# Retention, then a GEMM pair with ELU: eight weight sums and four scalings of v on VectorE instead of GpSimd

## The chip, the cores and the metric

The kernel runs on one core of a Trainium2 chip. The metric is the device time of one execution in microseconds (us), as the median over several executions. A smaller number is better. The engines are written as in the profile: PE is TensorE (matmul), PEld its weight load, DVE is VectorE, ACT is ScalarE, POOL is GpSimd, and SP issues the DMAs. L740 is line 740 of the kernel before.

## What is computed

```python
# q, k, v: (4 batches, 8 heads, 768 tokens, 64), all fp32
gamma = 1.0 - 2.0 ** (-5.0 - np.arange(H))
for t in range(S):
    state = gamma[None, :, None, None] * state + np.einsum('bhd,bhe->bhde', k[:, :, t], v[:, :, t])
    y[:, :, t] = scale * np.einsum('bhd,bhde->bhe', q[:, :, t], state)
x = y.transpose(0, 2, 1, 3).reshape(3072, 512)
h = x @ w_in                                         # w_in: 512 x 2048
g = np.where(h > 0.0, h, np.exp(np.minimum(h, 0.0)) - 1.0)
out = g @ w_out                                      # w_out: 2048 x 512
```

## The kernel before

The 3072 tokens are worked on in six blocks of 512 (`tb` 0 to 5). For each block the retention part makes x in chunks of 128 tokens (four to a block), then a first GEMM with `w_in` and ELU makes g, and a second GEMM with `w_out` makes the output. The first block multiplies plainly in its first GEMM; all later GEMMs use Strassen's scheme with seven products of half-size matrices, and some of these products are split once more into seven. Schedules are written out by hand: Python generators emit a few instructions at each `next`, and each engine executes its own in the order in which they were emitted.

The change lies in the first GEMM of the second block (`tb` = 1), at 135 to 190 us. `first(n)` (L728) makes column block n of four. Its order comes from `strassen` (L698): product 1 (bank a, copied by ACT at L690), product 2 (bank b, read by DVE at L695, which gives C11), 6 (a, copied), 7 (bank d), 5 (a, copied; DVE reads bank d and gives C22), then 3 (C12) and 4 (bank d, read by DVE, C21). A product is eight matmuls as the profile counts them. Bank a has two buffers, b and d one each. The loop over n interleaves neighbours: products 1 and 2 of n+1 go ahead of products 3 and 4 of n (`tail`), and 6, 7 and 5 of n+1 follow. Each result passes through `elu`: two steps on ACT (L477, L478) and one on DVE (L481), which is put off by one result. After C12 two DVE differences follow (L752).

Besides, DVE makes sums for later use in this loop, a step at a time: `combine_w_in` (L674), for the first GEMM's weights, in the loop's `sides`; and `combine_w_out` (L647), whose results `wi` are sent to memory. `combine_small(j)` (L810) makes four sums of weight quarters for product j = 2 or 3 of the first GEMM of the third and later blocks, where that product is itself split in seven ("M2" and "M3"). It makes them on POOL (L816), M2 after n = 0 and M3 after n = 2, into a tile `wi` of the pool `stage`, whose three buffers it shares with `combine_w_out` and the earlier weight loads. M3 needs all that `combine_w_in` makes. `hold` (L112) is a 1x1 copy on POOL that makes the tile wait for other data. `send_small` (L641) then queues the DMAs of these tiles on SP; M2 and M3 take one DMA of 1 MB each.

`load(m)` (L99) brings chunk m of q, k and v: the loop loads chunk 8 + n at its top, for the third block. `scale_v(m)` (L275) multiplies the v part by a power of gamma (L281): on DVE for chunks 0 and 1, on POOL for all others. The four chunks of the third block are scaled after the loop. Behind the loop `stage` is closed, and `ring` takes over its memory: 11 tiles `wq` of quarter weights that `fetch_small` (L791; DMAs at L799 and L804) brings from memory for the second GEMM (L953) and for the split products of later blocks (L865).

Of the kernel before, what the change touches and what calls it, by code (L numbers as in the profile page):

```python
# [18 lines left out]
def kernel(  # L19
# [32 lines left out]
    nc = tc.nc  # L52
# [12 lines left out]
    CPB = TB // C  # L65
# [33 lines left out]
    def load(m, parts=1):  # L99

        if m >= NCHUNK:
            return
        t = ldpool.tile([P, 2048], FP32, name="chunk", tag="chunk")
        raw[m] = (
            t[:, 0:1024].rearrange("p (a h c) -> p a h c", a=2, c=C),
            t[:, 1024:2048].rearrange("p (a h d) -> p a h d", a=2, d=D),
        )
        for part in range(parts):
            c = slice(part * 2048 // parts, (part + 1) * 2048 // parts)
            nc.sync.dma_start(t[:, c], qkv[m, :, c])  # L110

    def hold(t, other):  # L112

        if other is not None:
            nc.gpsimd.tensor_copy(t[0:1, 0:1], other[0:1, 0:1])
# [6 lines left out]
    w_a, w_b, w_s = ([x[:, n] for n in range(NQ)] for x in (w_a_, w_b_, w_s_))  # L122
# [100 lines left out]
    for h in range(H):  # L223
# [11 lines left out]
        out=causal, in_=causal, compare_op=ALU.is_gt, fill=1.0, base=0, pattern=[[-1, P]], channel_multiplier=1  # L235
# [36 lines left out]
    carry = [const.tile([P, HP, D], FP32, name=f"carry{n}") for n in range(2)]  # L272
    held = {}

    def scale_v(m):  # L275
        if m >= NCHUNK:
            return
        i = chunks[m][1]
        qk, kv = raw[m]
        eng = nc.vector if m < 2 else nc.gpsimd  # L280
        eng.tensor_tensor(  # L281
            out=kv[:, 1], in0=kv[:, 1], in1=vf[:, i].unsqueeze(2).to_broadcast([C, H, D]), op=ALU.mult
        )
# [80 lines left out]
    def outputs(tb, pp):  # L364

        y = [ps_r.tile([P, 2 * 2, 2, D], FP32, name="y", tag="r") for _ in range(2)]
        for x in range(2):
            for j in range(4):
                pt = raw[tb * CPB + 2 * pp + j // 2][0][:, 1].rearrange("p h c -> p (h c)")
                within(tb, pp, x, j, y, lambda p: pt[:, (x * HP + p) * D :][:, 0:D])  # L370
        for other in range(2):
            if not other:
                yield
            else:

                for sub in range(2):
                    seen = epool.tile([P, 8], FP32, name="seen", tag="seen")
                    nc.vector.tensor_copy(seen.rearrange("p (j x) -> p j x", x=2), y[sub][:, :, :, 0])
                yield
            for x in range(2):  # L380
                across(tb, pp, x, other, y)
        i = chunks[tb * CPB + 2 * pp][1]
        for sub in range(2):
            nc.vector.tensor_tensor(
                out=place_of(x_of(tb)[:, :, 2 * pp * C : 2 * (pp + 1) * C])[:, :, :, sub, :], in0=y[sub],
                in1=place_of(powers[:, :, i * C : (i + 2) * C])[:, :, :, sub, :], op=ALU.mult,
            )
# [26 lines left out]
    def outputs_of_first():  # L414

        y = [bank(x).rearrange("p a (b x d) -> p (a b) x d", b=2, x=2) for x in "bd"]
        for x in range(2):
            for j in range(4):
                pt = raw[x][0][:, 1].rearrange("p h c -> p (h c)")
                within(0, 0, x, j, y, lambda p: pt[:, ((j // 2) * HP + p) * D :][:, 0:D])  # L420
            yield
            across(0, 0, x, 0, y)
            for sub in range(2):
                if not fresh(0, 2 * x + sub):
                    seen = epool.tile([P, 8], FP32, name="seen", tag="seen")
                    nc.vector.tensor_copy(seen[:, 0:4], y[sub][:, :, x, 0])
            if x:
                yield
            across(0, 0, x, 1, y)
            if x:  # L430
                yield
            for sub in range(2):
                nc.vector.tensor_tensor(
                    out=place_of(xb[:, :, 0 : 2 * C])[:, :, x, sub, :], in0=y[sub][:, :, x],
                    in1=place_of(powers[:, :, 0 : 2 * C])[:, :, x, sub, :], op=ALU.mult,
                )
            if not x:
                yield
# [141 lines left out]
    def small_of_pieces(at):  # L580

        sources = [
            (decoded[2 * NQ + n].rearrange("p r (d c) -> p (r d) c", d=2)[:, 1:4], sums[n])
            for n in (2 * at, 2 * at + 1)
        ]
        return combine_w_out(at, *sources)
# [54 lines left out]
    def send_small():  # L641
        while to_send:
            nc.sync.dma_start(*to_send.pop(0))
# [84 lines left out]
    def first(n):  # L728

        a11, a12, s1, a22 = w_a[n][:, :, 0], w_a[n][:, :, 1], w_b[n][:, :, 0], w_b[n][:, :, 1]  # L730
        s2, s3, s4 = (w_s[n][:, j] for j in range(3))
        b11, b12, b21, b22 = (x_of(1)[:, 2 * r : 2 * r + 2, half[t]] for r in range(2) for t in range(2))
        t1, t2, t3, t4_ = xt1
        pairs = {1: (a11, b11), 2: (a12, b21), 3: (s4, b22), 4: (a22, t4_), 5: (s1, t1), 6: (s2, t2), 7: (s3, t3)}

        def product(j, ps, begin):
            w, x = pairs[j]
            for fi in range(2):
                for j2 in range(2):
                    nc.tensor.matmul(  # L740
                        ps[:, fi, :], lhsT=w[:, fi, j2, :], rhs=x[:, j2, :],
                        start=(begin and fi == 0 and j2 == 0), stop=(j2 == 1), skip_group_check=True,
                    )

        mine = lambda name: gq[name][:, 2 * n : 2 * n + 2, :]

        def use(name, h):
            flat = lambda x: x.rearrange("p a b -> p (a b)")
            elu(flat(mine(name)), flat(h))
            if name == "C12":  # L750

                sub = lambda o, x, y: nc.vector.tensor_tensor(out=o, in0=x, in1=y, op=ALU.subtract)  # L752
                later.append(lambda: sub(mine("T3"), mine("C22"), mine("C12")))
                later.append(lambda: sub(mine("T1"), mine("C12"), mine("C11")))

        return strassen(product, use, None)
# [50 lines left out]

    W_IN = {2: w_a_[:, :, :, 1], 3: w_s_[:, :, 2]}

    def combine_small(j, behind=None):  # L810

        t = stage.tile([P, 4, 4, P], FP32, name="wi", tag="stage")
        hold(t.rearrange("p k f d -> p (k f d)"), behind)
        a11, a12, a21, a22 = (W_IN[j][:, 2 * r : 2 * r + 2, :, c, :] for r in range(2) for c in range(2))
        s1, s2, s3, s4 = (t[:, k].rearrange("p (n f) c -> p n f c", f=2) for k in range(4))
        tt = lambda o, x, y, op: nc.gpsimd.tensor_tensor(out=o, in0=x, in1=y, op=op)  # L816
        tt(s1, a21, a22, ALU.add)
        tt(s2, s1, a11, ALU.subtract)
        tt(s3, a11, a21, ALU.subtract)
        tt(s4, a12, s2, ALU.subtract)  # L820
        to_send.append((scratch3[j - 1], t.rearrange("p k f d -> p (k f d)")))

# [289 lines left out]
    sc = [ps_r.tile([P, 2, HP, D], FP32, name="sc", tag="r") for _ in range(2)]  # L1112
    score_products(sc, 0, 0, 0)
    scale_v(0)
    mask_pair(sc, 0)
    unread(1, TH)
# [3 lines left out]
    y = outputs_of_first()  # L1120
# [7 lines left out]
    take()  # L1128
    take()
    scale_v(1)  # L1130
    mask_pair(sc, 1)
    inner = plain_first()
# [10 lines left out]
    take()  # L1143
    state_sum(kvs, 0, 0, 1, 1)
    scale_v(2)
    scale_v(3)
    prepare(2, by_vector=True)
# [12 lines left out]
    y = outputs(0, 1)  # L1160
# [9 lines left out]
    def run(steps):  # L1170
        for _ in steps:
            pass
# [8 lines left out]
    def some(steps, count):  # L1181
        for _ in itertools.islice(steps, count):
            pass

    for n, _ in enumerate(inner):
# [19 lines left out]
        elif n == 12:  # L1205
            smalls = small_of_pieces(0)
# [12 lines left out]
    for n in second_of_first():  # L1219
# [6 lines left out]
        elif n == 1:  # L1226
            smalls = small_of_pieces(1)
# [48 lines left out]
    sides = [  # L1276
        itertools.chain(combine_w_in(1), last), itertools.chain(combine_w_in(2), combine_w_in(3)), iter(()), iter(()),
    ]
    smalls = [2], [], [3], []
    for n in range(NQ):  # L1280
        load(2 * CPB + n)
        cur = first(n)
        for at in range(3):
            next(cur)

        for _ in tail:
            pass
        for s in cur:
            next(sides[n], None)
            next(sides[n], None)  # L1290
            if s == "gap":
                break
        for _ in sides[n]:
            pass
        tail = cur
        for j in smalls[n]:
            combine_small(j, w_s[1].rearrange("p s a b c -> p (s a b c)") if j == 2 else None)
        send_small()
    for m in range(2 * CPB, 3 * CPB):
        scale_v(m)  # L1300

    early.close()
    ring = ctx.enter_context(tc.tile_pool(name="ring", bufs=RING))
# [14 lines left out]
    for s in sec:  # L1318
        if s == "first":
            step += 1  # L1320
        at = (step, s if s in ("first", "middle") else "end")
# [7 lines left out]
    for tb in range(2, NTB):  # L1329
# [25 lines left out]
        for at, j in enumerate(TWICE):  # L1355
            cur = first_twice(tb, j)
# [120 lines left out]
```

## Time and profile before

| | |
|---|---|
| median of 3 runs (635.6 to 638.48) | 635.99 us |
| the profiled execution | 636.29 us |
| its span, first to last instruction | 634.4 us |
| start of the first product of the changed GEMM | 135.40 us |
| start of the second GEMM's first product | 182.14 us |
| start of the first split product in the third block's first GEMM (L865) | 244.25 us |

Busy time by stretch, from the same execution (us from the span's start; us of busy time):

| stretch | what runs | PE | DVE | ACT | POOL |
|---|---|---|---|---|---|
| 0 to 87.21 | first block's retention and first GEMM | 83.77 | 67.95 | 60.62 | 9.54 |
| 87.21 to 135.40 | first block's second GEMM | 48.19 | 42.20 | 16.05 | 0.00 |
| 135.40 to 190.30 | second block's first GEMM, start of its second | 53.73 | 44.80 | 26.28 | 17.49 |
| 190.30 to 244.25 | second block's second GEMM | 53.95 | 41.47 | 8.07 | 0.00 |
| 244.25 to 634.40 | the other four blocks | 387.10 | 285.33 | 141.87 | 13.53 |

A busy engine isn't necessarily the one that sets the pace of a stretch. In lists in order of time, a line has the start, the duration, the engine, the line of code, the operation with output and inputs, the shapes, and how many instructions are merged (x8); the bracket gives idle time ahead of it and the instruction that ended it. Merged durations run from the first start to the last end. In lists of waits a line has the waiter, what it waited for, the total in us, how often, and the longest.

### The profile page before, as it was taken

To read this page: it belongs to the slowest core of one execution; us is meant where nothing else is said; L and a number is where in the kernel's file an instruction comes from. 1 tells how busy PE (TensorE), PEld (TensorE's weight loads), DVE (VectorE), ACT (ScalarE), POOL (GpSimd) and SP (SyncE) were. 2 spreads that over 40 slices of the span, in tenths; PEclk is the share of its full clock that TensorE was granted. 3 is DMA by queue.
4 is the path that set the end of the run, shared out by engine and by line. 5 is a ranking of instruction groups with operands and counts; after the bars stand their busy time and mean duration, and the time that the engine had idled before them with its cause. 6 is when DMAs were issued, how large, how long until landed. Compare 5 with 4: busy or idle time off the path is not lost.

```text
span 634.4 us, 16149 instructions
## 1 busy us (share of the span) xinstructions
PE 626.7 (99%) x6680; PEld 560.7 (88%) x6680; DVE 481.7 (76%) x870; ACT 252.9 (40%) x472; POOL 40.6 (6%) x40
## 2 busy tenths in 40 slices
PE   8999999999999999999999999999999999999998
PEld 5764568888899999889999989999988999988997
DVE  5779979978879685589676598867489878558975
ACT  6599635014551113554112556111465311366311
POOL 1111000003600000200000100000110000000000
PEclk9999999999999999999999999999999999999999
DMA  8698867687477778504889701789820697700794
GB/s 336 264 390 307 269 205 222 189 248 258 176 239 228 242 254 272 239 2 135 277 267 312 290 4 55 258 283 286 302 100 4 218 299 236 238 24 2 231 309 158
DMA packets 75897, 136.85 MB, mean 216 GB/s; under 512 B 6320, under 2 KB 31792, under 8 KB 70704
## 3 DMA queue, kind: packets, MB, share of 16 engines
q1 hardware_dynamic: 75824, 135.82, 64.2%
q8 instruction: 53, 0.87, 0.5%
q14 instruction: 20, 0.16, 0.1%
HBM read 114.56 MB, written 21.23 MB: 214 GB/s over the span
## 4 chain that ended last, share of the span: by engine, by line
PE 94%; DVE 4%; issue 1%; ACT 0%; DVEq 0%
PE pa L953 20%; PE pa L911 10%; PE pd L953 10%; PE pb L953 5%; PE pa L865 5%; PE pb L911 4%; PE pa L521 3%; PE qa L911 3%; PE x L611 3%; PE pa L740 2%; PE pd L865 2%; PE qd L911 2%; PE pd L911 2%; PE pa L611 2%; PE y L394 2%; PE kv L338 2%
## 5 line engine op out<-in xcount | busy, mean ns | idle before, releaser
L961 ACT COPY ms<-pa 128x128 f32<-128x128 f32 x104 | 27.6, 265 | 147.1 <-PE pa L953 143.7
L953 PE MATMUL pa<-ts,wq 128*128 128x128 f32 x560 | 74.2, 275 | 0.0
L953 PE MATMUL pd<-ts,wq 128*128 128x128 f32 x552 | 73.6, 276 | 0.1
L953 PEld LDWEIGHTS pa<-ts,wq 128*128 128x128 f32 x560 | 68.5, 192 | 0.4
L953 PEld LDWEIGHTS pd<-ts,wq 128*128 128x128 f32 x552 | 67.1, 192 | 0.9 <-DVE res L965 0.5
L953 PE MATMUL pa<-gC,wq 128*128 128x128 f32 x480 | 64.6, 278 | 0.0
L478 ACT ACTIVATE r<-r 128x512 f32<-128x512 f32 x96 | 60.5, 631 | 3.0
L953 PEld LDWEIGHTS pa<-gC,wq 128*128 128x128 f32 x480 | 59.0, 192 | 1.3
L477 ACT ACTIVATE r<-gC 128x512 f32<-128x512 f32 x64 | 39.9, 624 | 32.0 <-DVE gC L919 32.0
L965 DVE TENSOR_TENSOR res<-pd,ms 128x128 f32<-128x128 f32 x68 | 19.4, 286 | 39.6 <-PE pd L953 38.4
L281 POOL TENSOR_TENSOR chunk<-chunk,vf 128x512 f32<-128x512 f32 x22 | 26.3, 1199 | 318.4 <-DMA chunk<-in_qkv_dram 153.5
L481 DVE SCALAR_TENSOR_TENSOR gC<-r,gC 128x512 f32<-128x512 f32 x64 | 44.3, 724 | 0.7 <-ACT r L478 0.7
L827 DVE TENSOR_TENSOR ts<-gC,ts 128x512 f32<-128x512 f32 x60 | 41.3, 688 | 1.0
L827 DVE TENSOR_TENSOR ts<-gC 128x512 f32<-128x512 f32 x60 | 40.9, 682 | 0.0
L953 PE MATMUL pb<-gC,wq 128*128 128x128 f32 x240 | 31.7, 275 | 0.0
L986 ACT COPY res<-pa 128x128 f32<-128x128 f32 x34 | 9.0, 265 | 55.1 <-PE pa L953 55.1
L953 PEld LDWEIGHTS pb<-gC,wq 128*128 128x128 f32 x240 | 29.2, 192 | 0.0
L690 ACT COPY m<-pa 128x512 f32<-128x512 f32 x24 | 13.9, 581 | 30.1 <-PE pa L911 14.2
L919 DVE TENSOR_TENSOR gC<-qa,gC 128x512 f32<-128x512 f32 x8 | 5.5, 692 | 25.1 <-PE qa L911 18.3
L911 PE MATMUL pa<-xt,w_s 128*128 128x256 f32 x96 | 23.0, 382 | 0.0
L911 PE MATMUL pa<-xt,w_b 128*128 128x256 f32 x96 | 23.0, 382 | 0.0
L965 DVE TENSOR_TENSOR res<-res 128x512 f32<-128x512 f32 (+1 forms) x31 | 20.6, 666 | 3.0 <-DVE res L965 0.5
(256 smaller groups left out, 1258.4 us busy)
## 6 DMA issues: line engine op xcount, KB each, us to landing
wq<-scratch_dram SPq DMA_DIRECT2D x277, 256.0 KB, 4.2
chunk<-in_qkv_dram SPq DMA_DIRECT2D x23, 1024.0 KB, 8.3
wraw<-in_w_dram SPq DMA_DIRECT2D x15, 1024.0 KB, 6.1
out_dram<-res SPq DMA_DIRECT2D x14, 256.0 KB, 3.8
scratch_dram<-gT SPq DMA_DIRECT2D x12, 256.0 KB, 4.2
scratch_dram<-m SPq DMA_DIRECT2D x12, 192.0 KB, 5.6
scratch_dram<-so SPq DMA_DIRECT2D x4, 512.0 KB, 4.8
scratch_dram<-wi SPq DMA_DIRECT2D x2, 1024.0 KB, 5.1
```

The costliest lines, as they stand in the source:

```text
L281: eng.tensor_tensor(out=kv[:, 1], in0=kv[:, 1], in1=vf[:, i].unsqueeze(2).to_broadcast([C, H, D]), op=ALU.mult)
L477: nc.scalar.activation(e, h, AF.Relu, scale=-1.0)
L478: nc.scalar.activation(e, e, AF.Exp, scale=-1.0)
L481: nc.vector.scalar_tensor_tensor(g, e, -1.0, h, ALU.add, ALU.max)
L521: nc.tensor.matmul(hp, lhsT=w[n][:, fi, j // 2, j % 2, :], rhs=xb[:, j, :], start=(j == 0), stop=(j == 3))
L611: nc.tensor.matmul(X[j][:, d, :], lhsT=w[j][:, d * P : d * P + P], rhs=x[j], start=(n == 0 and d == 0), stop=at_end, skip_group_check=True,)
L827: sub = lambda o, x, y: nc.vector.tensor_tensor(out=o, in0=x, in1=y, op=ALU.subtract)
L865: nc.tensor.matmul(ps[:, f, :], lhsT=lhs[f], rhs=xs[j][k], start=(begin and f == 0), stop=True, skip_group_check=True,)
L911: nc.tensor.matmul(ps[:, fi, :], lhsT=w[:, fi, j2, :], rhs=x[:, j2, :], start=(j in (1, 7) and fi == 0 and j2 == 0), stop=(j2 == 1), skip_ ...
L953: nc.tensor.matmul(ps, lhsT=w[:, f, :], rhs=ts[j][k][:, f, :], start=(begin and f == 0), stop=(f == 3), skip_group_check=True,)
L961: nc.scalar.copy(m, ps)
L965: nc.vector.tensor_tensor(out=o, in0=x, in1=y, op=ALU.add)
```

## The change

`combine_small` becomes a generator that yields after each of its first three sums, and its sums run on DVE; the `hold` copy goes. `scale_v` gets a switch that chooses DVE, and the four scalings for the third block move from behind the loop into its last turn. The steps are placed as follows: M2's first sum ahead of the loop, its second and third in turn n = 0, its fourth in turn 1; M3's first in turn 2 ahead of `tail`, its second and third later in that turn, its fourth at the turn's end; chunk 8's v in turn 3 ahead of `tail`, chunks 9 to 11 later in that turn. M2's DMA is thereby queued at the end of turn 1 and not of turn 0. Scalings of later blocks stay on POOL.

```diff
-    def scale_v(m):
+    def scale_v(m, by_vector=False):
...
-        eng = nc.vector if m < 2 else nc.gpsimd
+        eng = nc.vector if by_vector or m < 2 else nc.gpsimd
...
-    def combine_small(j, behind=None):
+    def combine_small(j):
 
         t = stage.tile([P, 4, 4, P], FP32, name="wi", tag="stage")
-        hold(t.rearrange("p k f d -> p (k f d)"), behind)
...
-        tt = lambda o, x, y, op: nc.gpsimd.tensor_tensor(out=o, in0=x, in1=y, op=op)
+        tt = lambda o, x, y, op: nc.vector.tensor_tensor(out=o, in0=x, in1=y, op=op)
         tt(s1, a21, a22, ALU.add)
+        yield
         tt(s2, s1, a11, ALU.subtract)
+        yield
         tt(s3, a11, a21, ALU.subtract)
+        yield
         tt(s4, a12, s2, ALU.subtract)
         to_send.append((scratch3[j - 1], t.rearrange("p k f d -> p (k f d)")))
...
-    smalls = [2], [], [3], []
+    smalls = {2: combine_small(2), 3: combine_small(3)}
+    some(smalls[2], 1)
     for n in range(NQ):
         load(2 * CPB + n)
         cur = first(n)
         for at in range(3):
             next(cur)
 
+        if n in (1, 2):
+            some(smalls[n + 1], 1)
+        elif n == 3:
+            scale_v(2 * CPB, True)
         for _ in tail:
             pass
-        for s in cur:
+        for at, s in enumerate(cur):
             next(sides[n], None)
             next(sides[n], None)
+            if at == 1 and n in (0, 2):
+                some(smalls[2 if n == 0 else 3], 2)
+            elif at == 1 and n == 3:
+                for m in range(1, CPB):
+                    scale_v(2 * CPB + m, True)
             if s == "gap":
                 break
         for _ in sides[n]:
             pass
         tail = cur
-        for j in smalls[n]:
-            combine_small(j, w_s[1].rearrange("p s a b c -> p (s a b c)") if j == 2 else None)
+        if n in (1, 2):
+            run(smalls[n + 1])
         send_small()
-    for m in range(2 * CPB, 3 * CPB):
-        scale_v(m)
```

## What is predicted, before the run

> **What bounds the kernel now.** I read the page's busy shares first, then the waits of TensorE, then the order of time of each engine in the stretch that the change touches (135 to 190 us), and the waits of the SP queue last.
>
> ```profile
> span 634.4 us, 16149 instructions
> PE 626.7 (99%) x6680; PEld 560.7 (88%) x6680; DVE 481.7 (76%) x870; ACT 252.9 (40%) x472; POOL 40.6 (6%) x40
> ```
>
> TensorE is busy for 99% of the span, and the chain that ended last is PE for 94%. So nothing that DVE or POOL saves counts by itself; only time in which TensorE stands idle in the touched stretch can be won. The PE waits name it:
>
> ```profile
> PE pd L740 <- DVE h L695: 1.2, 2, 0.7
> ```
>
> and the order of time of PE shows both places (start us, us, then engine, line, operation; the bracket is idle time and its releaser):
>
> ```profile
> 149.21 1.89 PE L740 MATMUL pd<-xb,w_b 128*128 128x256 f32 x8
> 150.94 1.89 PE L740 MATMUL pa<-xb,w_s 128*128 128x256 f32 x8
> 153.56 1.99 PE L740 MATMUL pd<-xb,w_s 128*128 128x256 f32 x8 [0.73 <-DVE h L695]
> 155.38 1.96 PE L740 MATMUL pa<-xb,w_b 128*128 128x256 f32 x8
> ...
> 164.09 1.89 PE L740 MATMUL pa<-xb,w_s 128*128 128x256 f32 x8
> 166.42 1.99 PE L740 MATMUL pd<-xb,w_s 128*128 128x256 f32 x8 [0.44 <-DVE h L695]
> 168.25 1.96 PE L740 MATMUL pa<-xb,w_b 128*128 128x256 f32 x8
> ```
>
> An undisturbed product of eight matmuls starts 1.727 us after the one before (149.21 to 150.94). The product `pd` is product 7 of column block n=1 (then n=2): it needs bank d, which frees when DVE has read product 4 of the block before (L695). It starts 2.62 us after its predecessor instead of 1.73, and the two products behind it come 0.09 and 0.07 late: 1.05 us. The second place costs 0.60 + 0.10 + 0.07 = 0.77 us. Check over the whole GEMM: its first product starts at 135.40, the second GEMM's first at 182.14; 26 products lie between, 26 x 1.727 = 44.90, and 46.74 - 44.90 = 1.84 us. That is all TensorE loses there: 0.29% of the span.
>
> Why DVE is late is in the same stretch:
>
> ```profile
> 145.63 1.73 POOL L816 TENSOR_TENSOR wi<-w_a 128x512 f32<-128x512 f32 x1
> 146.14 1.63 DVE L647 TENSOR_TENSOR wi<-w_s 128x384 f32<-128x384 f32 x1
> 147.31 1.58 POOL L816 TENSOR_TENSOR wi<-w_a,wi 128x512 f32<-128x512 f32 x1
> 147.81 1.51 DVE L647 TENSOR_TENSOR wi<-wi,w_s 128x384 f32<-128x384 f32 x1
> 149.24 0.54 DVE L647 TENSOR_TENSOR wi<-w_s 128x384 f32<-128x384 f32 x1
> ...
> 162.70 3.07 DVE L481 SCALAR_TENSOR_TENSOR gC<-r,h 128x512 f32<-128x512 f32 x2
> 165.69 0.68 DVE L695 TENSOR_TENSOR h<-pd,m 128x512 f32<-128x512 f32 x1
> 166.29 0.67 DVE L481 SCALAR_TENSOR_TENSOR gC<-r,pa 128x512 f32<-128x512 f32 x1
> ```
>
> The same 128x384 operation takes 1.63 and 1.51 us while a POOL sum runs and 0.54 us once POOL is done; the pair of L481 takes 3.07 us beside POOL sums (two of 0.69 elsewhere). The last two lines, one operand in PSUM, run beside POOL at full speed. These stretched operations stand right ahead of the two late reads of bank d.
>
> **What the Trainium skill says.** GPSIMD Engine Reference, "8. Key points": POOL shares its SBUF interfaces with VectorE, and contends with DVE instructions that have two SBUF inputs. The trace agrees, down to the PSUM exception just shown. The same page, "4.1 Engine selection", puts two-input elementwise work on POOL at about half DVE's speed; here the L816 sums take 1.27 to 1.73 us on POOL and the like L674 sums 0.69 on DVE. VectorE: DVE Perf Modes, "The TRN2 errata", gives an fp32 tensor_tensor as (N+151)/0.96 ns, 691 ns for 512; the trace has 0.68 to 0.69, starting 0.60 us apart when independent and 0.72 when one needs the last.
>
> **The change part by part.** Removed: one 1x1 copy, eight POOL sums, and four POOL scalings in this stretch (L281 at 168.09 to 176.57). With them goes what they cost DVE: 1.63-0.54, 1.51-0.54, 3.07-1.28, L752 1.69 and 1.41 against 0.69, L481 1.10 and 1.30 against 0.68: 6.6 us of DVE time. Added on DVE: 12 instructions of 0.60 to 0.72, some 8 us. DVE's total stays about level; what counts is where the pieces stand. I replay DVE with PE at 1.727 us a product (starts without the stalls: product 3 of n=0 147.48, 4 149.21, 6 of n=1 150.94, 7 152.67; for n=2 one block later 159.57, 161.30, 163.03, 164.75).
> - First sum of M2, before the loop's first product is added up: DVE idles 1.18 us before 139.12. Free.
> - Its second and third: DVE idles 1.66 us before 144.85, waiting for ACT; two cost 1.3. Free.
> - Four L647 then run 146.1 to 148.15 (4 x 0.46 to 0.57) instead of to 150.25. The read of product 2 (`h<-pb`) moves from 150.17 to 148.15. ACT needs 1.36 us for its two ELU steps (150.88 to 152.17 before), during which DVE does one L481 and the fourth M2 sum (to 150.0). The L481 that waits for ACT runs at 150.2 to 150.9, so DVE is free when product 4 ends at about 151.2, reads it by 151.9, and product 7 can start at 152.67 with some 0.6 us to spare. First stall gone: 1.05.
> - n=2: the L674 sums end at about 160.4, `h<-pb` at 161.0, L481, first M3 sum to 162.1, L481 behind ACT to 163.0, `h<-pd` 163.25 to 163.95, needed at 164.75. Second stall gone: 0.77, with 0.7 to spare.
> - Second and third M3 sums follow the L752 pair, ahead of an `h<-pd` that waits for ACT: nothing queued behind them is needed by TensorE at once.
> - Fourth M3 sum stands behind that `h<-pd`. ACT's copy of product 5 starts 0.2 us after it (168.41), the read 0.62 later (169.03), L481 169.64, the sum 170.25 to 170.95. POOL had ended M3 at 168.13. This is the one step that becomes later.
> - Four scalings of v: one behind an L481 in an ACT wait, three behind L752 at about 178.0, the last needing its chunk. Chunk 11's load stands behind M3's send in SP, so it is issued at about 171.35 and lands 6.9 us later as before (168.53 to 175.5), at 178.3; DVE gets to it at 179.2. The next `h<-pd` waits for ACT until about 181.1. Free, 1.2 us to spare.
> - SP: M2's send falls behind one chunk load instead of ahead of it; M2 is first multiplied at 244 us (L865), so no one waits. M3's send moves 168.16 to about 170.98, and what stands behind it counts:
>
> ```profile
> 168.16 0.33 SPq L643 DMA_DIRECT2D scratch_dram<-wi  x1
> 168.53 0.42 SPq L110 DMA_DIRECT2D chunk<-in_qkv_dram  x1
> 173.01 0.80 SPq L804 DMA_DIRECT2D wq<-scratch_dram  x2
> ...
> SPq L804 <- DMA scratch_dram<-wi: 3.9, 1, 3.9
> ```
>
> The ring of `wq` weights lies over the `stage` buffers, so the first fetch waits until M3's send has landed: 173.01, 4.85 us after its issue; that fetch lands 4.4 us later (the DMA view of that moment), at 177.4. TensorE first loads it at 181.9: a cover of 4.5 us. After: 170.98 + 4.85 + 4.4 = 180.23, while TensorE would want it at 181.9 - 1.84 = 180.06. The cover is used up, a new stall of about 0.2 us. The second fetch is 0.37 behind and lands after some 4.8, at 181.0, just when wanted; the third is wanted only at 185.5.
>
> Sum: -1.05 - 0.77 + 0.2 = -1.6 us. The profiled execution took 636.29 us (span 634.4 and 1.9 around it) and so becomes 634.7; the median shown, 635.99, is 0.3 under that execution, so I state 634.4. Nothing after 190 us is touched: from there the order on PE, ACT and DVE is the same, and what is won moves through to the end.
>
> **Rivals.**
> - A, the new wait takes it back. If M3's send comes 1 to 2 us later than I reckon, TensorE waits as long for its first `wq`, and each us is lost one for one: 635.4 to 636. For: the cover is exactly used up. Against: in the replay the chain to the send is set by PE and ACT, not by DVE's load.
> - B, DVE itself is the bound there: the L647 and L481 were slow from something other than POOL (DMA traffic), or the 12 new pieces fill what was freed, and both stalls stay: 636.0. For: DVE was busy 37.55 of 46.74 us. Against: the 0.54 the moment POOL ends.
> - C, slower: the first GEMM's new M3 order makes the `wq` ring start late by more than the stalls were worth. The place is the first product at 180.3; the point is an M3 send after 170.8 + 1.84 = 172.6, from which on every us is a loss. DVE sums at 1.0 us instead of 0.65 would put it some 3 us late (173.9): 3.1 - 1.84 = +1.3, 637.3. Beyond 0.5% it would have to come after 176, for which I see no reason.
> - D, faster by more than 0.5%: needs 3.2 us, where TensorE loses only 1.84. Only idleness hidden in the modelled matmul ends would allow it: 632.5.
>
> **How the numbers follow.** Forecast 0.70, A 0.11, B 0.08, C 0.07, D 0.04. The forecast's own bounds: all of 1.84 won without a new wait gives 634.15; with 1 us of new wait 635.1. The three runs shown lie 2.9 us apart, so the range takes 1 us beyond these at the fast end, and A and B and the start of C at the other: 633.0 to 636.8. Half a percent, 3.2 us, is about what a measurement of this kernel can tell from no change; forecast, A, B and most of C lie inside it. Faster 0.06 (D and scatter), slower 0.05 (the end of C and scatter), within 0.89.
>
> **What would show it.** In the profile of the changed kernel: no `DVE h L695` wait on PE `pd` of L740; the four L647 at 0.54 each; the first L953 product near 180.3 to 180.5; M3's send near 171 and the first `wq` fetch near 175.9. A wait of L953 on the `wq` DMA of over 0.5 us is A or C; the old stalls still there, with L647 at 1.5 us, is B. I am wrong if a product of 135 to 182 us waits for a DVE read at a place where it did not before, or if the time between 190 us and the end changes by more than a few tenths.

## The result, and the profile after

The changed kernel takes 635.1 us in the median of 20 runs (633.43 to 637.31), the kernel before 636.45 beside it: a ratio of 0.9976, 95% interval 0.9964 to 0.9987, or 1.5 us less (0.8 to 2.3). That lies within half a percent, the bound used in the prediction, and in these runs its sign is clear of the scatter. One execution measured further below, the profiled one of e3_pool_beside, took 918.13 us at a granted clock of 0.656; the ratios leave it out, and e3_again has the profile that is read instead.

The page of the changed kernel, its first lines:

```profile
span 634.7 us, 16136 instructions
PE 626.1 (99%) x6680; PEld 561.2 (88%) x6680; DVE 482.9 (76%) x882; ACT 253.2 (40%) x472; POOL 22.4 (4%) x27
```

The span of this one execution (it took 637.01 us in all) is not shorter than that of the one before. DVE has 12 instructions more and yet only 1.2 us more busy time; POOL has lost 18 us. To see the gain one has to look at the stretch, in the order of time of PE:

```profile
151.63 1.89 PE L740 MATMUL pd<-xb,w_b 128*128 128x256 f32 x8
153.35 1.89 PE L740 MATMUL pa<-xb,w_s 128*128 128x256 f32 x8
155.08 1.89 PE L740 MATMUL pd<-xb,w_s 128*128 128x256 f32 x8
156.81 1.89 PE L740 MATMUL pa<-xb,w_b 128*128 128x256 f32 x8
...
163.71 1.89 PE L740 MATMUL pd<-xb,w_b 128*128 128x256 f32 x8
165.44 1.89 PE L740 MATMUL pa<-xb,w_s 128*128 128x256 f32 x8
167.17 1.89 PE L740 MATMUL pd<-xb,w_s 128*128 128x256 f32 x8
...
182.71 1.05 PE L955 MATMUL pa<-gC,wq 128*128 128x128 f32 x8
```

Both brackets `<-DVE h L695` are gone; every product starts 1.727 us after the last. The first product starts at 137.81 and the second GEMM's at 182.71: 44.90 us, where it was 46.74. From there to the end of the span it is 452.0 us, before 452.3. What hides the gain in this execution is the start: 137.81 against 135.40. PE's waits show where that came from, in the first block, ahead of everything that the change touches:

```profile
PE y L394 <- DVE chunk L350: 1.5, 1, 1.5
PE pa L1106 <- DVE blank L208: 1.4, 1, 1.4
PE sc L307 <- DMA chunk<-in_qkv_dram: 0.6, 1, 0.6
```

The 1.5 and the 0.6 were not among PE's waits of before. The 0.6 is an input chunk that landed late; behind the 1.5 the chain of waits goes back through DVE and ACT to a load of weights (`wraw`, L142) that landed at 65.6 us. So a single profile, or a single time, can't show 1.8 us here; the stretch can, and so do many runs.

DVE in order of time, ahead of the first of the two places:

```profile
148.47 0.55 DVE L647 TENSOR_TENSOR wi<-w_s 128x384 f32<-128x384 f32 x1
149.06 0.56 DVE L647 TENSOR_TENSOR wi<-wi,w_s 128x384 f32<-128x384 f32 x1
...
151.67 0.68 DVE L815 TENSOR_TENSOR wi<-w_a,wi 128x512 f32<-128x512 f32 x1
152.51 0.69 DVE L481 SCALAR_TENSOR_TENSOR gC<-r,h 128x512 f32<-128x512 f32 x1 [0.16 <-ACT r L478]
153.56 0.69 DVE L695 TENSOR_TENSOR h<-pd,m 128x512 f32<-128x512 f32 x1 [0.35 <-PE pd L740]
```

L647 takes 0.55 us and no more 1.5 to 1.6, and the last line has turned round: DVE now waits for PE at bank d, not PE for DVE. The moved M2 sum (L815) stands inside DVE's wait for ACT.

### The profile page after: what moved, and what is told of

Its sections match the earlier page's. It is cut to its first block, busy times and chain, and to the rows that moved or that the text cites. A ratio compares the mean times of both kernels' runs of the same rounds, so it can differ in the third digit from the quotient of the medians.

```text
span 634.7 us, 16136 instructions
## 1 busy us (share of the span) xinstructions
PE 626.1 (99%) x6680; PEld 561.2 (88%) x6680; DVE 482.9 (76%) x882; ACT 253.2 (40%) x472; POOL 22.4 (4%) x27
## 4 chain that ended last, share of the span: by engine, by line
PE 92%; DMA 3%; DVE 2%; ACT 2%; issue 1%; SPq 0%; DVEq 0%
PE pa L955 20%; PE pa L913 10%; PE pd L955 10%; PE pb L955 5%; PE pa L867 5%; PE pb L913 4%; PE pa L740 4%; PE qa L913 3%; PE x L611 3%; DMA wraw<-in_w_dram 3%; PE pd L867 2%; PE qd L913 2%; PE pd L913 2%; PE pd L740 2%; PE pa L611 2%; PE y L394 2%
## 5 line engine op out<-in xcount | busy, mean ns | idle before, releaser
L481 DVE SCALAR_TENSOR_TENSOR gC<-r,gC 128x512 f32<-128x512 f32 x64 | 44.7, 730 | 0.7 <-ACT r L478 0.7
L281 POOL TENSOR_TENSOR chunk<-chunk,vf 128x512 f32<-128x512 f32 x18 | 20.6, 1147 | 431.8 <-DMA chunk<-in_qkv_dram 226.2
L921 DVE TENSOR_TENSOR gC<-qa,gC 128x512 f32<-128x512 f32 x8 | 5.5, 691 | 25.1 <-PE qa L913 18.3
L913 PE MATMUL pa<-xb,w_a 128*128 128x256 f32 x96 | 22.7, 379 | 0.0
```

The source lines that it names most:

```text
L281: eng.tensor_tensor(out=kv[:, 1], in0=kv[:, 1], in1=vf[:, i].unsqueeze(2).to_broadcast([C, H, D]), op=ALU.mult)
L481: nc.vector.scalar_tensor_tensor(g, e, -1.0, h, ALU.add, ALU.max)
L913: nc.tensor.matmul(ps[:, fi, :], lhsT=w[:, fi, j2, :], rhs=x[:, j2, :], start=(j in (1, 7) and fi == 0 and j2 == 0), stop=(j2 == 1), skip_ ...
```

## The experiments

"Stretch" is the time from the first product of the changed GEMM to the first of the second GEMM in the run's profile. Ratios are to the kernel before on the same chip, with 95% intervals.

| run | what it is | stretch, us | ratio |
|---|---|---|---|
| before | | 46.74 | 1 |
| after | the change | 44.90 | 0.9976 (0.9964 to 0.9987) |
| after_again | the change | 45.07 | 0.9988 (0.9974 to 1.0002) |
| e1_sums_only | sums on DVE, scalings on POOL | 45.00 | 0.9959 (0.9940 to 0.9977) |
| e1_again | the same | 45.09 | 0.9959 (0.9942 to 0.9975) |
| e2_scalings_only | sums on POOL, scalings on DVE | 46.72 | 1.0000 (0.9986 to 1.0013) |
| e3_pool_beside | the change and unread POOL sums | see e3_again | 1.0006 (0.9995 to 1.0017) |
| e3_again | the same | 48.78 | 1.0006 (0.9990 to 1.0022) |
| e4_late_send | M3's send 2.9 us later | 45.61 | 0.9988 (0.9977 to 0.9999) |
| e5_later_send | M3's send later still | 50.36 | 1.0080 (1.0055 to 1.0105) |
| e6_all_on_dve | every scaling on DVE | 45.99 | 1.0599 (1.0563 to 1.0634) |
| e7_early_m2 | before, M2 on POOL earlier | 45.40 | 0.9985 (0.9972 to 0.9998) |
| e8_dve_when_landed | scalings of later blocks on DVE, late | 44.89 | 1.0033 (1.0019 to 1.0047) |
| e9_e1_with_fillers | e1 and four tiny DVE copies | 45.42 | 0.9977 (0.9963 to 0.9991) |

**Which half of the change does it: e1 and e2.** e1 puts the scalings back on POOL behind the loop:

```diff
-        elif n == 3:
-            scale_v(2 * CPB, True)
...
-            elif at == 1 and n == 3:
-                for m in range(1, CPB):
-                    scale_v(2 * CPB + m, True)
...
         send_small()
+    for m in range(2 * CPB, 3 * CPB):
+        scale_v(m)
```

> The eight sums of M2 and M3 on DVE as in the change, the four scalings of v on POOL behind the loop as before. I measure the stretch from the start of the changed GEMM's first product to the start of the second GEMM's first product: 46.74 us before, 44.90 after the change. If the POOL sums beside DVE's late reads of bank d were the cause, this kernel has 44.9 to 45.3 (the scalings, now free to start as soon as their chunks land, may stretch one DVE operation each) and runs within 0.5 us of the changed kernel. If the scalings on POOL were what held DVE up, at least half of the 1.84 us comes back: 45.8 or more.

e2 is the reverse: the kernel before, with those scalings alone put on DVE at the places that the change gives them.

> Only the four scalings of v move to DVE; the sums stay on POOL. If the POOL sums are the cause, both waits for bank d stay (0.7 and 0.4 us of idle PE) and the stretch is 46.7 us, the time that of the kernel before. If the scalings were, the stretch falls to about 45.

e1 has the whole gain in the stretch, e2 none of it. In e2's order of time both waits are where they were, and as long:

```profile
152.66 1.99 PE L740 MATMUL pd<-xb,w_s 128*128 128x256 f32 x8 [0.72 <-DVE h L695]
165.51 1.99 PE L740 MATMUL pd<-xb,w_s 128*128 128x256 f32 x8 [0.43 <-DVE h L695]
```

The sums are the cause; moving the scalings wins nothing there. In e1 the scalings on POOL still stretch a DVE operation each (an L674 beside one took 1.56 us), and PE loses 0.1 us at the second place, where an L481 of 0.93 us stands ahead of the read of bank d. The time of e1 was expected within 0.5 us of the changed kernel's and came out lower by about 1 us in the ratios; more on this below.

**Contention, or DVE's order: e3 and e7.** e3 adds POOL sums to the changed kernel whose results nobody reads, four after turn 0 and four after turn 2:

```diff
+    spare = so_[:, 0, 0:2]
+
+    def beside(n):
+        x = w_s[n][:, 2].rearrange("p a b c -> p a (b c)")
+        for _ in range(4):
+            nc.gpsimd.tensor_tensor(out=spare, in0=x, in1=x, op=ALU.add)
...
+        if n in (0, 2):
+            beside(n + 1)
         send_small()
```

> The changed kernel, with eight further POOL sums of the same size whose results nobody reads, at about the times at which POOL made M2 and M3 before. Contention theory: DVE's L647 goes back from 0.55 to 1.5 us beside them and the pair of L481 to about 3 us; the bank d waits return, and as DVE now also has the sums, the stretch is 46.7 to 47.7 us, no better than before. If the DVE operations were slow from DMA traffic, or the gain came from the order of DVE's work alone, the stretch stays at 44.9.

> e3_pool_beside once more, for its profile: L647 at about 1.5 us beside the extra POOL sums, the bank d waits back, the stretch 46.7 to 47.7 us by the contention theory; 44.9 by the rival.

The profile is e3_again's. POOL in order of time, the second group of unread sums:

```profile
161.93 5.38 POOL L1287 TENSOR_TENSOR so<-w_s 128x512 f32<-128x512 f32 x4 [14.03 <-DVE w_s L674]
```

DVE beside it:

```profile
163.44 1.52 DVE L815 TENSOR_TENSOR wi<-w_s 128x512 f32<-128x512 f32 x1
164.89 1.52 DVE L481 SCALAR_TENSOR_TENSOR gC<-r,h 128x512 f32<-128x512 f32 x1
166.33 0.68 DVE L695 TENSOR_TENSOR h<-pd,m 128x512 f32<-128x512 f32 x1
```

and the waits of PE:

```profile
PE pd L740 <- DVE h L695: 2.3, 2, 1.5
...
PE pa L955 <- DMA wq<-scratch_dram: 0.7, 1, 0.7
```

With POOL busy and nothing else changed, the two-input operations take 1.5 us again, the one that reads bank d (PSUM) keeps its 0.68, and the waits are back. The stretch came out 1.1 us above the upper end expected: the waits are longer than before (0.85 and 1.48 us) because DVE now carries the M3 sum there as well, and the late DVE also delayed M3's send, so that PE waited for `wq`. Of the four L647, expected at 1.5 us each, only one was stretched (1.39 us): the M2 sums ahead of them, at 1.53 and 1.52 us, met most of the first group.

e7 is the other proof, from the kernel before. The sums stay on POOL, and M2's four are only issued earlier (and without their `hold` copy, which e3 leaves out too):

```diff
             some(held["last"], 3)
+            combine_small(2)
...
-    smalls = [2], [], [3], []
+    smalls = [], [], [3], []
```

> The kernel before, with all sums and scalings on POOL, but M2's four sums issued some 10 us earlier, at the end of the first block's second GEMM. If the first wait for bank d (1.05 us with its tail) comes from POOL's M2 sums stretching L647, it goes and the second one (0.77) stays: stretch 45.5 to 45.9 us. If POOL's place doesn't matter, 46.7.

POOL makes M2 at 109.6 to 116.2 us there. The first wait is gone, as expected, and the second is down to a trace, which was not, so that the stretch, 45.40 us, lies just under the range:

```profile
150.70 1.89 PE L740 MATMUL pa<-xb,w_s 128*128 128x256 f32 x8
152.43 1.89 PE L740 MATMUL pd<-xb,w_s 128*128 128x256 f32 x8
...
162.79 1.89 PE L740 MATMUL pa<-xb,w_s 128*128 128x256 f32 x8
164.57 1.99 PE L740 MATMUL pd<-xb,w_s 128*128 128x256 f32 x8
```

The M3 sums still stretch the pair of L481 (3.12 us) in e7, but DVE enters that place undelayed, and its read of bank d comes just in time (164.57, 0.05 us late; with the two products behind it the stretch loses 0.22 us there). Most of the second wait was the first one's lateness, handed on. The rest of e7's 0.50 us is at its start, where an L595 of the first block's end waited for a DMA of `gT`:

```profile
133.53 0.69 DVE L595 TENSOR_TENSOR gT<-x,m 128x512 f32<-128x512 f32 x1 [2.01 <-DMA scratch_dram<-gT]
```

That is the price of the new place. Beside POOL's M2 sums at 109.6 to 116.2 us three L540 of DVE took 1.57 to 1.66 us and an L191 1.75, all 0.69 in the kernel before, and the first of the `gT` DMAs was issued 2.5 us later (130.08 against 127.55). M2's own send can't have held it up: it was issued at 138.76, after all of these had landed.

**How much cover the `wq` ring has: e4 and e5.** e4 puts M3's fourth sum and its send off:

```diff
         elif n == 3:
+            run(smalls[3])
+            send_small()
             scale_v(2 * CPB, True)
...
-        if n in (1, 2):
-            run(smalls[n + 1])
-        send_small()
+        if n == 1:
+            run(smalls[2])
+        if n < 2:
+            send_small()
```

> The changed kernel, with M3's fourth sum and its DMA put off into the last turn, ahead of the scaling of chunk 8 and behind the load of chunk 11: about 2.9 us later. In the changed kernel the first wq landed 0.8 us ahead of its use (181.7 against 182.5). If the wq ring hangs on M3's send as predicted, PE now waits for the wq DMA for about 2.1 us (1.2 to 2.3, since the chunk's load now goes ahead), the stretch is 46.1 to 47.2 us and the gain is gone. If the ring has cover from elsewhere, the stretch stays at 44.9.

e5 has the same two lines behind the last turn's L752 pair, ahead of the scalings of chunks 9 to 11.

> As e4, but M3's fourth sum and its DMA come after the last turn's L752 pair, about 4.8 us later than in e4. With a cover that is used up, each further us should cost one: PE waits about 5.5 us (0.7 + 4.8) for the first wq, the stretch is 49.9 to 50.6 us, the time some 5.5 us above the changed kernel's and 0.4 to 0.7% above the one before. If e4's short wait was a limit of something else (PE busy on other work, fetches reordered), the wait stays under 2 us.

First e4's start of the second GEMM, then e5's, in PE's order of time:

```profile
180.28 1.13 PE L955 MATMUL pa<-gC,wq 128*128 128x128 f32 x8 [0.55 <-DMA wq<-scratch_dram]
```

```profile
185.09 2.05 PE L955 MATMUL pa<-gC,wq 128*128 128x128 f32 x8 [5.30 <-DMA wq<-scratch_dram]
```

The ring does hang on M3's send, and e5 is slower than the kernel before. e4's wait is much shorter than expected, and most of the gain is still there. Its send was 2.91 us later in the stretch, as meant, but no chunk was under way beside it any more: from the send to the first fetch it took 3.97 us (4.65 in the changed kernel) and the fetch landed in 2.7 us instead of 3.7. These two give back 1.7 us. The cover was smaller than the 0.8 us of the expectation: PE's load of the weights starts 0.4 us behind the landing in e4 and e5, where it waits for nothing else, so about 0.4 us was left. The sum 2.91 - 0.68 - 1.0 - 0.4 = 0.8 fits that load, which comes 0.90 us later in the stretch than in the changed kernel; 0.55 us of it shows as idle time of PE. Between e4 and e5, where neither has a chunk beside it, 4.8 us of delay cost 4.75 us of stretch: one for one.

**POOL's contention elsewhere: e6 and e8.** e6 takes POOL out of all scalings:

```diff
-        eng = nc.vector if by_vector or m < 2 else nc.gpsimd
+        eng = nc.vector
```

> The changed kernel, with every scaling of v on DVE, those of the second, fourth, fifth and sixth block too. After the second GEMM of the second block has begun PE waits for nothing in the trace, so taking POOL's contention away there should bring nothing: within 0.5 us of the changed kernel, if the first block (where the second block's chunks are scaled and PE waits 3 us in all) is no better or worse. If contention with POOL costs wherever it is, about 1 us or more is won.

A clear miss: 6% slower. DVE's waits and PE's:

```profile
DVE chunk L281 <- DMA chunk<-in_qkv_dram: 53.0, 13, 8.6
```

```profile
PE pa L867 <- DVE gC L881: 16.1, 3, 5.7
PE pd L867 <- DVE res L967: 10.4, 3, 3.9
```

In the later blocks the scaling is issued directly behind its chunk's load. On POOL it waits there for the chunk and holds nobody up. On DVE it stands in the queue of all that PE's banks wait for. The expectation counted DVE's busy time and forgot what stands behind a waiting instruction. e8 keeps the second block's scalings on POOL and issues the others only when the chunks have landed:

```diff
                 load((tb + 1) * CPB + n)
-                scale_v((tb + 1) * CPB + n)
...
                 elif n == 1 and more:
+                    for m in range(CPB):
+                        scale_v((tb + 1) * CPB + m, True)
                     retention_step(tb + 1, 0)
```

> In e6 DVE waited 53 us in all for chunks still under way, with PE's work queued behind. Here the scalings for the fourth to sixth block are on DVE too, but all four are issued together in the turn n = 1 of the first GEMM's rest, where POOL had the last chunk scaled some 4 us earlier; the second block's stay on POOL. If the wait for the DMA in DVE's queue was e6's loss, DVE waits for no chunk there and the time is within 2 us of the changed kernel (three times 2.4 us of DVE work, beside PE). If DVE has no room for the scalings at all, most of e6's loss stays: 660 us or more.

The DMA wait was e6's loss: 37 of the some 40 us by which e6 was above the changed kernel are gone (676.18 to 639.32, medians of two chips). The rest is more than expected, 3.6 us above the changed kernel's 635.73 beside it; PE waits 3.4 us in three places for an L921 that stands behind the four scalings. DVE had no room there for four of them in a row.

**The changed kernel and e1 side by side.**

> The changed kernel once more, beside e1 on one chip: stretch 44.9 us, no wait for the first wq, 0.2 to 0.3% under the kernel before. Its first product of the changed GEMM may start anywhere from 134.5 to 138 us, as the profiles up to now had it, and the time should follow that start.

> e1 once more, beside the changed kernel: stretch 45.0 us and the time within 0.15% of the changed kernel's, since the scalings on POOL cost PE 0.1 us there. If e1's first result (0.41% under the kernel before) was more than scatter, it is again 0.15% or more ahead.

The changed kernel missed both of its expectations: it was 0.12% under the kernel before, with an interval that reaches no change, and its stretch was 45.07 us, because PE waited a little for the first `wq` (see "The new wait for `wq`" below). Its time didn't follow its start of 135.65 either: this execution took 637.06 us. e1 came out 0.41% under before again and so ahead of the changed kernel (14 of its 16 executions are under 635 us, 4 of 22 of the changed kernel's), though its stretch is not shorter. e9 asks whether that comes from the scalings:

```diff
+        elif n == 3:
+            nc.vector.tensor_copy(lng[0:1, 0:1], lng[0:1, 1:2])
...
+            elif at == 1 and n == 3:
+                for m in range(1, CPB):
+                    nc.vector.tensor_copy(lng[0:1, 0:1], lng[0:1, 1:2])
```

> e1 was 0.41% under the kernel before twice, the changed kernel 0.24% and 0.12%, though PE loses 0.1 us more in e1's changed stretch. e9 is e1 with four 1x1 copies on DVE where the changed kernel has its four scalings, so that DVE's number and order of instructions is the changed kernel's while the scalings stay on POOL. If the scalings on DVE are what costs the changed kernel its distance, e9 is like e1: 0.35 to 0.45% under before. If it is where the instructions lie in DVE's program, e9 is like the changed kernel: 0.1 to 0.25% under before. The stretch is 45.0 us in either case.

e9 is at 0.9977, like the changed kernel, with the scalings on POOL: that speaks, weakly, against the scalings and for the place of the instructions in the program. Its interval overlaps e1's, and in its profile PE waited 0.36 us for the first `wq`. It stays open why e1 is ahead. What the profiles show of the scatter lies in two places outside the changed stretch: the first product of the changed GEMM starts between 134.5 and 138.1 us in the runs that leave the first block as it was, after input chunks and weights that land earlier or later; and in some executions, those of after_again, e2 and e5 among them, PE halts in the fourth block's retention within a run of 64x64 matmuls, for nothing that the profile shows:

```profile
303.27 0.34 PE L409 MATMUL y<-chunk 64*64 64x64 f32 x5 [1.80 <-issue]
```

e1 is the fastest version found, by its two results ahead of the change by 0.2 to 0.3%; only the result is shown, not a cause.

## The prediction against the runs

- **What bounds.** Right: PE's idle time in the stretch was the whole stake, 1.84 us, and all of it was won in the first profile (44.90, the sum of 26 products), 1.67 us in the second (45.07). DVE's busy time, up by 1.2 us, didn't matter.
- **The cause.** Right: e3 brings the waits back by POOL work alone, e7 takes the first away, and most of the second, by moving POOL work alone, e2 keeps them. Rival B falls. One thing the prediction had not separated: it priced the second wait as POOL's M3 sums' work; e7 shows that it needed the first wait's lateness too.
- **The replay of DVE.** With the later start of 2.41 us taken off, the reads of product 4 start at 151.15 and 163.23 (replayed 151.2 and 163.25), the fourth M3 sum at 170.24 (170.25), the three last scalings at 177.97 (178.0). Pricing each moved piece at its neighbours' start-to-start distance was enough.
- **The new wait for `wq`.** Its mechanism is right (e4, e5). Its 0.2 us was absent in the first profile and there in the second, and the working behind it was off in two ways. M3's send came at 170.95 in the old times, as reckoned. The prediction then carried over the old times for its landing and for the fetch, 4.85 and 4.4 us; they took 4.65 and 3.7. And it took the weights as ready once they land. In the profiles in which PE waited for them (after_again, e1_again, e3_again, e4, e5, e6, e9) PE's load started 0.4 to 0.5 us behind the landing, so the changed kernel's 0.8 us between the two were 0.4 of cover. In after_again, with its send at the same point of the stretch, the fetch took 4.1 us and nothing was left:

```profile
180.69 0.97 PEld L955 LDWEIGHTS pa<-gC,wq 128*128 128x128 f32 x8 [0.39 <-DVE chunk L281]
```

  The view names a scaling as what ended the wait; e1_again, which has no scaling on DVE there, waited in the same way. The product came 0.17 us late, which is what its stretch is longer by. In the five profiles with this send (after, e8, after_again, e9, e6) PE lost 0, 0, 0.17, 0.5 and 1.1 us at this place. What scatters with it is chunk 11, which is loaded between the send and the fetch: it took 7.3, 7.3, 8.0, 8.4 and 9.0 us, and the first fetch landed 0.6 to 0.7 us after it each time. So the forecast of 0.2 us lies within what these five profiles lost, but partly by luck.
- **The time.** -1.6 us was forecast and 1.5 us came out in the ratio. That they agree to a tenth is luck: the interval runs from 0.8 to 2.3 us, and the second set of runs gave 0.8. The sentence that nothing after 190 us is touched holds in the first profile (452.0 us from the second GEMM's first product to the end, against 452.3). In after_again it is 454.1, 1.80 of it the halt shown above; e2 has such a halt too (1.25 us), with the sums on POOL as before, and why it comes is open. One execution can't show the gain in its time: the first 138 us scatter by more.
- **Rivals A and C.** Their mechanism is what e4 and e5 make; in the change itself the send came 1.7 us ahead of C's point (172.6).

## What to carry to other kernels

Before moving work from POOL to DVE, look for DVE operations that take two to three times their usual time while POOL runs (here those with two SBUF inputs, and in e7 the L191 with one): freeing those can pay for the moved work, and only the ones ahead of a read that PE waits for count. Don't put an instruction that waits for a load into the queue of an engine that empties PE's banks (e6: 6%); issue it once the data has landed, where that engine waits anyway (the changed stretch), and not four in a row where it doesn't (e8: 3.6 us). When a buffer pool takes over another's memory, its first load waits for the last send out of it, so the latest of the old pool's sends sets a date for the next stage.

## What the runs showed of the hardware

A long wait of PE costs more than its length. e5 waited 5.3 us once, but lost some 2.5 us more behind it. Busy time by stretch of e5, with the granted clock behind POOL's column:

```profile
core 0: us, PE busy (x) PEld busy (x) DVE busy (x) ACT busy (x) POOL busy (x), PEclk, DMA share, GB/s
179.80:185.09 5.29, 0.00 (x1) 0.03 (x1) 3.88 (x6) 1.85 (x3) 0.00 (x0) 0.83 0.66 230
185.09:187.00 1.91, 1.91 (x9) 1.91 (x10) 0.00 (x0) 0.00 (x0) 0.00 (x0) 0.50 0.70 181
187.00:190.00 3.00, 3.00 (x13) 2.73 (x13) 0.89 (x2) 0.27 (x1) 0.00 (x0) 0.50 1.00 338
190.00:195.00 5.00, 5.00 (x33) 4.58 (x32) 1.94 (x3) 2.28 (x5) 0.00 (x0) 0.99 0.76 291
```

The clock fell to 0.50 during the wait: the mean of 0.83 over 5.29 us means 3.5 us at full clock and 1.8 at half. PE started again at 185.09, and the clock stayed at 0.50 until 190.1, for 5.0 us in which PE did half its usual work: some 2.5 us lost. The order of time agrees: the first three products behind the wait started 1.84, 1.70 and 2.47 us apart, where the changed kernel has 0.89, 0.89 and 1.73. The Trainium skill says so too (TensorE: Matmul & The Clock Gate, "Part 1: The HAM clock gate"): after an idle window of about 3.4 us the array drops to half its clock, and it takes about as long a busy one to come back; here it dropped after 3.5 us and came back after 5.0. The waits of 0.4 to 1.5 us in e3_again, e4 and e9 left the clock at 1.00. By the ratios e5 is 6.6 us above the changed kernel (7.4 by the medians), where 5.5 were expected. Its longer stretch and the slow clock come to 8.0 us in this execution; the intervals of the ratios are too wide to tell these sums apart, so it is the trace that shows the extra 2.5.
